# Attention with decay and a gated feed-forward layer: GpSimd's products kept away from VectorE's scaling, and ScalarE's casts spread out

## The chip, the cores and the metric

The kernel runs on one core of a Trainium2 chip. The metric is the device time of one execution in microseconds (us), as the median over runs. The engines are called as in the profile: PE is TensorE's matmul (PEld its weight load), DVE is VectorE, ACT is ScalarE, POOL is GpSimd, SP is SyncE.

## The reference

There are 8 batches of 8 heads with 576 positions of 64 numbers, so 4608 tokens of 512 numbers. A causal attention with a decay from running sums of `s` is followed by a normalization and a gated feed-forward layer:

```python
scores = scale * q @ k.T                              # per batch and head, scale = 1/8
cum    = cumsum(maximum(s, 0))
scores = where(causal, -1e9, scores + minimum(-(cum[i] - cum[j]), 0))
attn   = softmax(scores)
x      = (attn @ v) as rows of 512                    # 4608 x 512
xn     = x / sqrt(mean(x*x) + 1e-6) * rms_g
g      = xn @ w_gate                                  # 512 x 1536
out    = (g * sigmoid(g) * (xn @ w_val)) @ w_out      # 1536 x 512
```

## The kernel before

The feed-forward layer works in 9 chunks of 512 tokens, numbered 0 to 8. `ffn` emits a chunk. For each of 12 blocks of 128 columns it issues four matmuls for G (line 910), a tanh T on ACT (line 913), four matmuls for V (line 919), and on DVE first U from T and G (line 922), then Ht from U and V (line 915). After that come four output tiles of 12 matmuls each (line 932), taken out by ACT (line 937). G, V, the output tiles and part of the scores take turns in four PSUM buffers with the name `psF`, in the order in which they are asked for. A new G or V can therefore start only when the reader of the buffer's last use is done: for G's buffer that is U, for V's it is Ht.

The attention of the later batches is fitted in between by a planner that runs when the program is written. After every four matmuls of `ffn` it calls `step`, and each call is a slot, 36 of them in a chunk. In a slot the planner issues what is due by counts of slots alone. Nothing in it reacts to times on the chip. Each engine then works through its own instructions in the order in which they were issued, and waits at semaphores where data is not there.

For batches 4 to 7, a pair (b, c) is batch b and its block c of 128 positions. These are the steps that matter here:

- ScalarE casts Q to bf16 in five pieces (`cast_x`, lines 161 and 150). They stand in the queue `act_cast`. When all are done, SP's queue transposes K and Q piece by piece (`kq_dma`, line 189).
- A score run (`s_run`, matmuls of line 366) uses a `psF` buffer, a `psT` and a `psS`. In the next four slots ACT takes exponentials (line 379), and POOL sets the masked half to zero (line 383; for batches up to 3 it is line 318).
- POOL multiplies a block of V by the decay (`fold_b`, lines 402 and 405). I call this a fold. All tensors of it lie in SBUF.
- PE multiplies probabilities and V (`av_step`, lines 430 and 436), and DVE divides by the sums (lines 444 and 446), which gives a block of x.
- ACT squares the block and sums the squares (line 453). POOL makes the factor `al_all` out of the sum (`alpha`, lines 466 and 469). DVE scales the block by that factor and by `rms_g` (`x_scale`, line 476, inputs and output in SBUF). SP's queue transposes it into the feed-forward layer's input (line 487).

In `step` the parts come in this order: delayed work, one exponential, the scaling, casts on ACT, transposes, loads of V, then POOL's own queue or a fold, and last PE's work of the attention (`place`). The lines that decide on casts and folds are:

```python
        if not busy and not run_side(act_side) and last["run"] > 0:
            run_side(act_cast)
        ...
            if not run_side(pool_side) and phase() < 25 and not moved and fold_seq and ready(9, "V", *fold_seq[0]) and not (
                    scaled[0] < len(x_list) and ready(XLAG - 2, "AV", *x_list[scaled[0]], 1)):
                fold_b(*fold_seq.pop(0))
```

`ready(n, "AV", b, qb, 1)` is true from n slots after the second half of that block's product with V. `XLAG` is 6, `SQLAG` is 2, `MB` is 4. For batches up to 3 the factor is issued in the slot of the product; for later ones it comes three slots after it. `x_list[scaled[0]]` is the next block that DVE will scale.

Of the kernel before, what the change touches and what calls it, by code (L numbers as in the profile page):

```python
# [9 lines left out]
BF16 = mybir.dt.bfloat16  # L10
# [16 lines left out]
def kernel(  # L27
# [12 lines left out]
    nc = tc.nc  # L40
    B, H, S, D = q.shape
    DM = H * D
# [4 lines left out]
    NSC = 5  # L47
# [6 lines left out]
    def rows(c):  # L54
        return 128 if c < 4 else 64
# [14 lines left out]
    mp = fast.enter_context(tc.tile_pool(name="mp", bufs=1))  # L70
# [14 lines left out]
    MB = 4  # L85
    PERIOD, PACE, MLAG, XLAG, SQLAG = 9, 2, 1, 6, 2
# [4 lines left out]
    NX = 4  # L91
    x_sb = mp.tile([128, NX, DM], BF16, name="x_sb")
    xs_sb = mp.tile([128, NX, DM], BF16, name="xs_sb")
# [5 lines left out]
    g_col = mp.tile([128, CC], FP32, name="g_col")  # L99
    ss_all = mp.tile([128, B * NSC], FP32, name="ss_all")  # L100
    al_all = mp.tile([128, B * NSC], FP32, name="al_all")
    acc = mp.tile([128, 2560], BF16, name="acc")
    mag = mp.tile([128, H * 320], BF16, name="mag")
    s_sb = mp.tile([BH, S], FP32, name="s_sb")
# [12 lines left out]
    def psAV():  # L117
        return pp.tile([128, 512], FP32, name="psAV", tag="AV", bufs=1)
# [7 lines left out]
    def psT32():  # L126
        return pp.tile([128, 512], FP32, name="psT32", tag="T", bufs=1)
# [210 lines left out]
    def s_run(b, kb):  # L338
# [49 lines left out]
        def part(g, par):  # L388
            exps(g, par)
            if g:  # L390
                last[("RA", "RT")[par]] = slot[0]
            if par:
                after(MLAG, lambda: mask(g, kb, 0, 128))
                if join:
                    after(MLAG, lambda: mask(g, 4, 192, 64))

        last["RA"] = last["RT"] = 10 ** 6
        exp_q.extend((join, lambda a=(g, par): part(*a)) for g in (1, 0) for par in (0, 1))

    def fold_b(b, c):  # L400
        i = (b - MB) * H
        nc.gpsimd.tensor_tensor(
            out=v_sb[:, b % 2, c, :, 0:64], in0=v_sb[:, b % 2, c, :, 0:64],
            in1=vwx[:, c, i:i + H].unsqueeze(2).to_broadcast([128, H, 64]), op=ALU.mult)
        nc.gpsimd.tensor_copy(out=v_sb[:, b % 2, c, :, 64], in_=vwx[:, c, i:i + H])
        done["W", b, c] = slot[0]
# [6 lines left out]
    def part_of(b, qb):  # L413

        return slice(64, 128) if b >= MB and qb == 4 else slice(0, rows(qb))

    def av_step(b, qb, g, ps=None, act=False):
        p = b % 2
        if ps is None:
            ps = psT32() if 0 < b < MB and g == 1 else psAV()  # L420
        for j in range(4):
            h = 4 * g + j
            o = ps[:, j * NV:(j + 1) * NV]
            e, back, own = j, 128, 0
            if b >= MB:
                e = 2 * (j % 2) + j // 2
                if qb == 4:
                    back, own = 64, 128
            if qb > 0:
                nc.tensor.matmul(o, lhsT=E[:, eslot[b, qb - 1, g], e, back:back + 128],  # L430
                                 rhs=v_sb[:, p, qb - 1, h, :], start=(j == 0), stop=False)
            if qb < 4 or b >= MB:
                d = E[:, eslot[b, qb, g], e, own:own + 128]
            else:
                d = E[:, eslot[b, 4, 0]].rearrange("p h (a n) -> p (h a) n", n=128)[:, h, :]
            nc.tensor.matmul(o, lhsT=d, rhs=v_sb[:, p, qb, h, :],  # L436
                             start=(j == 0 and qb == 0), stop=(j == 3))
        if qb > 0:
            eread[eslot[b, qb - 1, g]] -= 1
        eread[eslot[b, qb, g if qb < 4 or b >= MB else 0]] -= 1  # L440
        R = part_of(b, qb)
        pv = ps[:, 0:4 * NV].rearrange("p (h e) -> p h e", e=NV)
        rZ = mp.tile([128, 4], FP32, name="rZ", tag="rZ", bufs=3)
        nc.vector.reciprocal(out=rZ[R], in_=pv[R, :, 64])  # L444
        xo = x_sb[R, (b * NSC + qb) % NX, :]
        nc.vector.tensor_tensor(  # L446
            out=xo[:, g * 256:(g + 1) * 256].rearrange("p (h d) -> p h d", h=4),
            in0=pv[R, :, 0:64], in1=rZ[R].unsqueeze(2).to_broadcast([R.stop - R.start, 4, 64]), op=ALU.mult)

        def norm(whole=True):  # L450
            col = b * NSC + qb
            if act:
                nc.scalar.activation(  # L453
                    out=xs_sb[R, (b * NSC + qb) % NX, :], in_=xo, func=AF.Square,
                    accum_out=ss_all[R, col:col + 1])
            else:
                nc.vector.scalar_tensor_tensor(
                    out=xs_sb[R, (b * NSC + qb) % NX, :], in0=xo, scalar=1.0, in1=xo,
                    op0=ALU.mult, op1=ALU.mult, accum_out=ss_all[R, col:col + 1])
            if whole:  # L460
                alpha(col, col + 1, R)
        return norm
# [58 lines left out]
    slot = [0]  # L521
    first, chunk = [0], [0]
    done = {}
    exp_q = []
    last = {"XS": -9, "P": -9, "RA": -9, "RT": -9, "run": -9, "S": -9, "AV": -9, "T": -9, "X": -9, "AVT": -9, "L": -9, "TT": -9, "TA": -9, "AVA": -9}
    s_seq = [(b, kb, g) for b in range(B) for kb in range(NSC) for g in (0, 1) if kb < 4 or g == 0]
    s_seq.sort(key=lambda x: (1, 0, x[2], x[1]) if x[0] == 1 and x[1] < 2 else (x[0], x[1], x[2], 0))
    s_seq = [x for x in s_seq if x[0] < MB or x[1] < 4 and x[2] == 0]
# [11 lines left out]
    pool_side, dve_side, v_side, act_side, act_cast = [], [], [], [], []  # L540
    x_seq = []
    fold_seq = [(b, c) for b in range(MB, B) for c in range(NSC)]

    def at(*key):
        return done.get(key, 10 ** 6)

    def ready(lag, *key):
        return at(*key) + lag <= slot[0]

    def run_side(queue):  # L550
        if queue and queue[0][0]():
            queue.pop(0)[1]()
            return True
        return False
# [22 lines left out]
    def phase():  # L577

        return slot[0] - first[0]
# [219 lines left out]
    def by_pe(b, qb):  # L799

        return b == 0 or (b, qb) in ((1, 2), (1, 3))
# [9 lines left out]
    scaled = [0]  # L811
    x_list = [(b, qb) for b in range(B) for qb in range(NSC)]
# [7 lines left out]
    def step(bare=False, tanh=False):  # L820

        slot[0] += 1
        while pending:
            pending.pop(0)()
        for x in [x for x in delayed if x[0] <= slot[0]]:
            delayed.remove(x)
            x[1]()
        busy = bool(exp_q) and phase() <= 24
        for _ in range(1):
            if exp_q:  # L830
                exp_q.pop(0)[1]()
        moved = False
        if scaled[0] < len(x_list):
            b, qb = x_list[scaled[0]]
            if ready(5 if (b, qb) == (1, 1) else XLAG if b >= MB else 3, "AV", b, qb, 1):
                x_scale(b, qb)
                last["XS"] = slot[0]
                scaled[0] += 1
                if not by_pe(b, qb):
                    assert xt_seq[0] == (b, qb)  # L840
                    xt_dma(*xt_seq.pop(0))
                    done["XT", b, qb] = slot[0] + 4
                    moved = True
        if not busy and not run_side(act_side) and last["run"] > 0:
            run_side(act_cast)

        if not moved and x_seq and slot[0] - last["X"] >= 2 and not (
                scaled[0] < len(x_list) and x_list[scaled[0]] != (1, 4) and ready(1 if x_list[scaled[0]][0] < MB else XLAG - 2, "AV", *x_list[scaled[0]], 1)):
            b, w, c = x_seq[0]
            old = ("R", b - 2, c) if b - 2 >= (XB if w else KB) else ("S", b - 2, 4, 0)  # L850
            if (ready(1 if b == 2 else 2, "cast", b, 1) and ready(1, *old)
                    and (w == 1 or ready(7, "K", b, c))):
                x_seq.pop(0)
                kq_dma(b, w, c)
                done["X", b, w, c] = last["X"] = slot[0]
                if b >= KB and (w, c) == (0, NSC - 1) and b + 2 < B:
                    casts(b + 2)
        bare = bare or chunk[0] == 0 and 30 <= phase() <= 33
        if slot[0] % 2 and not bare and not (chunk[0] == 0 and phase() >= 24):
            run_side(v_side)  # L860
        if not bare:
            if not run_side(pool_side) and phase() < 25 and not moved and fold_seq and ready(9, "V", *fold_seq[0]) and not (
                    scaled[0] < len(x_list) and ready(XLAG - 2, "AV", *x_list[scaled[0]], 1)):
                fold_b(*fold_seq.pop(0))
        place()
        if chunk[0] < 3 or last["AV"] < slot[0] and not moved:
            run_side(dve_side)
# [157 lines left out]
    with tc.manual_schedule():  # L1025
# [7 lines left out]
        for w in (0, 1):  # L1033
# [8 lines left out]
            out=mneg.rearrange("p (j n) -> p j n", j=2), in_=mneg.rearrange("p (j n) -> p j n", j=2),  # L1042
# [353 lines left out]
```

## Time and profile before

| | us |
|---|---|
| median of 3 runs | 364.1 |
| the runs | 364.74, 362.69, 364.10 |
| the profiled execution | 363.98 |
| its span, first to last instruction | 362.3 |
| PE busy in the span | 346.8 (96%) |
| DVE busy | 278.7 (77%) |
| ACT busy | 223.9 (62%) |
| POOL busy | 193.7 (53%) |

The span is what the profile's views divide up. In a row of the timeline the first number is the start in us from the span's beginning, the second the length, then engine, line, operation, and output<-input; an idle time before it and who ended it may stand in brackets. In a row of busy time by stretch come the stretch, its length, and the busy time of PE, PEld, DVE, ACT and POOL with the number of instructions, then the clock that PE was granted (1.00 is full speed), and the share and rate of the DMA.

### The profile page before, as it was taken

The page shows a single profiled execution, that of the slowest core. Times are in us where ns is not written, and L with a number is a line of the kernel's source. Part 1 is how long each engine was busy: PE and PEld are TensorE (multiplying, and loading weights), DVE is VectorE, ACT ScalarE, POOL GpSimd, SP SyncE. Part 2 cuts the span into 40 slices and gives each one's busy share as a digit, 9 for nine tenths or more (in the row PEclk, how much of TensorE's full clock was granted, in tenths as well). Part 3 has the DMA queues.
Part 4 walks back from the last instruction along what each step waited for, and adds up shares of the span by engine and source line. Part 5 has one row for each costly group of instructions (what it writes and reads, how often), then busy time and mean ns, then how long its engine had stood idle before and what let it go on. Part 6 is the DMA issues. An engine that isn't in the chain of part 4 may idle for free. (4 is left out here: it accounts for less than half of the span.)

```text
span 362.3 us, 6904 instructions
## 1 busy us (share of the span) xinstructions
PE 346.8 (96%) x2419; PEld 165.1 (46%) x2419; DVE 278.7 (77%) x524; ACT 223.9 (62%) x507; POOL 193.7 (53%) x310
## 2 busy tenths in 40 slices
PE   5989999999999999979999999999999999999993
PEld 2445444543444444434544444445444454444441
DVE  6797988698999888788769976997799359827820
ACT  3988885778787876845757845664666455223311
POOL 6959663738863878947583778565652210000000
PEclk9999999999999999989999999999999999999998
DMA  7999999999999599959996999299501221020011
GB/s 227 138 234 253 175 174 253 181 206 193 175 161 208 55 104 127 181 59 180 218 211 68 82 144 197 37 97 137 119 16 24 72 74 23 2 87 29 1 60 63
DMA packets 124800, 45.68 MB, mean 126 GB/s; under 512 B 103924, under 2 KB 119800, under 8 KB 124760
## 3 DMA queue, kind: packets, MB, share of 16 engines
q0 software_dynamic: 62368, 13.11, 45.2%
q1 hardware_dynamic: 51328, 23.67, 32.3%
q10 hardware_dynamic: 11064, 8.41, 9.9%
q8 instruction: 20, 0.33, 0.4%
q14 instruction: 20, 0.16, 0.2%
HBM read 37.90 MB, written 9.44 MB: 131 GB/s over the span
## 5 line engine op out<-in xcount | busy, mean ns | idle before, releaser
L919 PE MATMUL psF<-xnT,wv_sb 128*128 128x512 bf16 x432 | 111.9, 382 | 2.4 <-DVE U L922 2.4
L910 PE MATMUL psF<-xnT,wg_sb 128*128 128x512 bf16 x432 | 111.7, 381 | 0.3 <-ACT xnT L503 0.3
L913 ACT ACTIVATE T<-psF 128x512 f32<-128x512 f32 x108 | 64.4, 597 | 63.2 <-PE psF L910 60.7
L932 PE MATMUL psF<-wout_sb,Ht 128*128 128x512 bf16 x432 | 100.4, 379 | 0.0
L922 DVE SCALAR_TENSOR_TENSOR U<-T,psF 128x512 bf16<-128x512 f32 x108 | 73.8, 683 | 24.8 <-ACT T L913 22.7
L915 DVE TENSOR_TENSOR Ht<-U,psF 128x512 bf16<-128x512 bf16 x99 | 67.7, 684 | 6.1 <-PE psF L919 0.5
L919 PEld LDWEIGHTS <-wv_sb 128*128 128x128 bf16 x432 | 39.7, 98 | 47.4 <-issue 6.3
L932 PEld LDWEIGHTS <-Ht 128*128 128x128 bf16 x432 | 39.7, 98 | 44.4 <-issue 1.0
L910 PEld LDWEIGHTS <-wg_sb 128*128 128x128 bf16 x432 | 38.7, 98 | 41.4 <-issue 4.3
L937 ACT ACTIVATE osb<-psF 128x512 f32<-128x512 f32 x36 | 21.6, 600 | 48.3 <-PE psF L932 40.4
L309 ACT ACTIVATE E<-psS,biasK 128x256 bf16<-128x256 f32 (+3 forms) x136 | 44.7, 421 | 4.2 <-PE psS L285 4.0
L383 POOL TENSOR_SCALAR_AFFINE_SELECT E<-E 128x512 bf16<-128x512 bf16 (+1 forms) x40 | 24.9, 631 | 38.4 <-ACT E L379 35.7
L476 DVE SCALAR_TENSOR_TENSOR xs_sb<-x_sb,al_all,g_row 128x512 bf16<-128x512 bf16 (+1 forms) x36 | 31.4, 873 | 7.1 <-POOL al_all L469 6.8
L193 POOL DMA_DIRECT2D v_sb<-in_v_dram x40 | 35.2, 882 | 0.0
L318 POOL TENSOR_SCALAR_AFFINE_SELECT E<-E 128x512 bf16<-128x512 bf16 x28 | 19.3, 690 | 24.0 <-ACT E L309 23.3
L466 POOL TENSOR_SCALAR al_all<-ss_all 128x1 f32<-128x1 f32 (+2 forms) x39 | 10.7, 273 | 38.7 <-ACT xs_sb L453 31.0
L514 DVE TENSOR_TENSOR acc<-acc,mag 128x1280 bf16<-128x1280 bf16 x32 | 28.8, 923 | 0.3
L453 ACT ACTIVATE xs_sb<-x_sb 128x512 bf16<-128x512 bf16 (+1 forms) x37 | 23.2, 627 | 7.8 <-DVE x_sb L446 6.9
L446 DVE TENSOR_TENSOR x_sb<-psAV,rZ 128x256 bf16<-128x256 f32 (+1 forms) x61 | 25.9, 424 | 2.1
L436 PEld LDWEIGHTS <-E 128*128 128x128 bf16 x320 | 21.9, 98 | 10.4 <-issue 0.8
L469 POOL TENSOR_TENSOR al_all<-al_all,mhalf 128x1 f32<-128x1 f32 (+2 forms) x39 | 24.7, 633 | 3.2
L444 DVE RECIPROCAL rZ<-psAV 128x4 f32<-128x4 f32 (+1 forms) x61 | 10.9, 179 | 18.8 <-PE psAV L436 18.4
(135 smaller groups left out, 392.8 us busy)
## 6 DMA issues: line engine op xcount, KB each, us to landing
out_dram<-osb SPq DMA_DIRECT2D x36, 256.0 KB, 2.3
kq<-in_q_dram ACTq DMA_DIRECT2D x5, 1024.0 KB, 7.8
v_sb<-in_v_dram POOLq DMA_DIRECT2D x32, 128.0 KB, 4.8
kq<-in_k_dram SPq DMA_DIRECT2D x4, 512.0 KB, 5.8
kq<-in_q_dram SPq DMA_DIRECT2D x4, 512.0 KB, 7.6
kq<-in_k_dram ACTq DMA_DIRECT2D x2, 1024.0 KB, 9.3
kqn<-in_k_dram POOLq DMA_DIRECT2D x16, 128.0 KB, 4.9
wout_sb<-in_moe_w_out_dram POOLq DMA_DIRECT2D x2, 768.0 KB, 10.5
```

The source lines that it names most:

```text
L193: nc.gpsimd.dma_start(out=v_sb[0:n, b % 2, c, :, 0:64], in_=v[b, :, c * 128:c * 128 + n, :].rearrange("h p d -> p h d"))
L309: nc.scalar.activation(out=eo, in_=ei, func=AF.Exp, scale=0.125, bias=biasK[:, kb, bh:bh + 1])
L383: nc.gpsimd.affine_select(out=Ev, in_=Ev, pattern=[[0, 4], [1, nq]], compare_op=ALU.is_ge, fill=0.0, base=0, channel_multiplier=-1)
L446: nc.vector.tensor_tensor(out=xo[:, g * 256:(g + 1) * 256].rearrange("p (h d) -> p h d", h=4), in0=pv[R, :, 0:64], in1=rZ[R].unsqueeze(2). ...
L476: nc.vector.scalar_tensor_tensor(out=xs_sb[R, (b * NSC + qb) % NX, :], in0=x_sb[R, (b * NSC + qb) % NX, :], scalar=al_all[R, col:col + 1], ...
L514: nc.vector.tensor_tensor(out=acc[:, sl], in0=acc[:, sl], in1=mag[:, sl], op=ALU.max)
L910: nc.tensor.matmul(Gp, lhsT=wg_sb[:, cc, fs], rhs=xnT[:, cc, x0:x0 + DM], start=(cc == 0), stop=(cc == CC - 1))
L913: nc.scalar.activation(out=T, in_=Gp, func=AF.Tanh, scale=0.5)
L915: nc.vector.tensor_tensor(out=Ht[:, fb - 1, :], in0=pend[0], in1=pend[1], op=ALU.mult)
L919: nc.tensor.matmul(Vp, lhsT=wv_sb[:, cc, fs], rhs=xnT[:, cc, x0:x0 + DM], start=(cc == 0), stop=(cc == CC - 1))
L922: nc.vector.scalar_tensor_tensor(out=U, in0=T, scalar=1.0, in1=Gp, op0=ALU.add, op1=ALU.mult)
L932: nc.tensor.matmul(Op, lhsT=Ht[:, fb, tb * 128:(tb + 1) * 128], rhs=wout_sb[:, fb, :], start=(fb == 0), stop=(fb == FB - 1))
```

## The change

Three things change in `step`.

- A fold is no longer issued between a block's factor and its scaling. For a block of batches up to 3, folds are held back from the slot after its product with V; for later ones from two slots after it (it was four slots after, for all).
- A fold that is issued less than four slots after a scaling has a small copy ahead of it on POOL. The copy reads one element of the scaled row, so POOL waits there until DVE has done that scaling. 19 of the 20 folds have one.
- ScalarE's casts of Q are issued in every second slot at most, and not in the slot of a square sum or the one after. Before, they could go in each slot.

```diff
+    probe = mp.tile([128, 1], BF16, name="probe")
...
+    def behind_scale():
+        b, qb = x_list[scaled[0] - 1]
+        r0 = part_of(b, qb).start
+        nc.gpsimd.tensor_copy(out=probe[r0:r0 + 1], in_=xs_sb[r0:r0 + 1, (b * NSC + qb) % NX, DM - 1:DM])
...
             if act:
+                last["SQ"] = slot[0]
                 nc.scalar.activation(
...
-        if not busy and not run_side(act_side) and last["run"] > 0:
-            run_side(act_cast)
+        if not busy and not run_side(act_side) and last["run"] > 0 and slot[0] - last["C"] > 1 and slot[0] - last["SQ"] > 1:
+            if run_side(act_cast):
+                last["C"] = slot[0]
...
-            if not run_side(pool_side) and phase() < 25 and not moved and fold_seq and ready(9, "V", *fold_seq[0]) and not (
-                    scaled[0] < len(x_list) and ready(XLAG - 2, "AV", *x_list[scaled[0]], 1)):
+            if not run_side(pool_side) and phase() < 25 and not moved and fold_seq and ready(
+                    9, "V", *fold_seq[0]) and not (scaled[0] < len(x_list) and ready(
+                        0 if x_list[scaled[0]][0] < MB else SQLAG, "AV", *x_list[scaled[0]], 1)):
+                if slot[0] - last["XS"] < 4:
+                    behind_scale()
                 fold_b(*fold_seq.pop(0))
```

Since all later decisions of the planner follow from earlier ones, the order of the attention's instructions differs from the first fold of batch 4 on (chunk 3) to the end of chunk 7. The instructions are the same, apart from the 19 copies.

More of the change, by code (lines that the diff above doesn't have):

```diff
@@ L524 @@
     exp_q = []
-    last = {"XS": -9, "P": -9, "RA": -9, "RT": -9, "run": -9, "S": -9, "AV": -9, "T": -9, "X": -9, "AVT": -9, "L": -9, "TT": -9, "TA": -9, "AVA": -9}
+    last = {"C": -9, "SQ": -9, "XS": -9, "P": -9, "RA": -9, "RT": -9, "run": -9, "S": -9, "AV": -9, "T": -9, "X": -9, "AVT": -9, "L": -9, "TT": -9, "TA": -9, "AVA": -9}
     s_seq = [(b, kb, g) for b in range(B) for kb in range(NSC) for g in (0, 1) if kb < 4 or g == 0]
```

## The prediction

> **What bounds the kernel now.** I read the page's first two parts, then the busy time chunk by chunk, then the chain of waits, then the timeline around the one wait of TensorE that matters.
>
> ```profile
> span 362.3 us, 6904 instructions
> PE 346.8 (96%) x2419; PEld 165.1 (46%) x2419; DVE 278.7 (77%) x524; ACT 223.9 (62%) x507; POOL 193.7 (53%) x310
> PEclk9999999999999999989999999999999999999998
> ```
> TensorE (PE) is the bound: 96% busy, and the granted clock dips in one slice in the middle. The change adds and removes no matmul, so it can win only where PE idles or is slowed. The chunks say where (PE busy is the first figure after the length):
>
> ```profile
> 145.10:184.90 39.80, 37.38 (x251) 17.68 (x250) 31.56 (x51) 25.21 (x53) 28.16 (x45) 0.96 1.24 168
> 184.90:221.00 36.10, 36.09 (x266) 17.56 (x264) 29.70 (x55) 23.40 (x48) 25.36 (x39) 1.00 1.14 122
> 221.00:257.20 36.20, 36.20 (x267) 17.60 (x266) 29.95 (x55) 20.86 (x43) 23.31 (x39) 1.00 0.98 111
> ...
> PE psF L919 <- DVE U L922: 2.4, 1, 2.4
> ```
> The chunks from 184.9 on have PE filled. The chunk from 145.1, the first that the edits reach, has 2.42 us of idle PE and a mean clock of 0.96. The last line, from the chain of waits, is that idle time: one wait, by the V matmuls of line 919 for the U of line 922 on VectorE (DVE). The timeline there, engine by engine:
>
> ```profile
> 150.74 1.03 PE L910 MATMUL psF<-xnT,wg_sb 128*128 128x512 bf16 x4
> 152.47 1.03 PE L910 MATMUL psF<-xnT,wg_sb 128*128 128x512 bf16 x4
> 153.43 0.28 PE L366 MATMUL psF<-kqT 64*128 64x256 bf16 x1
> ...
> 153.66 0.38 PE L366 MATMUL psS<-kqT 64*128 64x256 bf16 x4
> 156.46 1.02 PE L919 MATMUL psF<-xnT,wv_sb 128*128 128x512 bf16 x4 [2.42 <-DVE U L922]
> ...
> 152.03 0.69 DVE L915 TENSOR_TENSOR Ht<-U,psF 128x512 bf16<-128x512 bf16 x1
> 152.63 3.18 DVE L476 SCALAR_TENSOR_TENSOR xs_sb<-x_sb,al_all,g_row 64x512 bf16<-64x512 bf16 x1
> 155.74 0.67 DVE L922 SCALAR_TENSOR_TENSOR U<-T,psF 128x512 bf16<-128x512 f32 x1
> ...
> 151.40 0.21 POOL L405 CAST v_sb<-vwx 128x8 bf16<-128x8 f32 x1
> 151.70 0.18 POOL L466 TENSOR_SCALAR al_all<-ss_all 64x1 f32<-64x1 f32 x1
> 151.97 0.56 POOL L469 TENSOR_TENSOR al_all<-al_all,mhalf 64x1 f32<-64x1 f32 x1
> 152.50 0.62 POOL L383 TENSOR_SCALAR_AFFINE_SELECT E<-E 128x512 bf16<-128x512 bf16 x1
> 153.10 1.03 POOL L402 TENSOR_TENSOR v_sb<-v_sb,vwx 128x512 bf16<-128x512 bf16 x1
> 154.09 0.21 POOL L405 CAST v_sb<-vwx 128x8 bf16<-128x8 f32 x1
> 154.24 1.03 POOL L402 TENSOR_TENSOR v_sb<-v_sb,vwx 128x512 bf16<-128x512 bf16 x1
> 155.22 0.67 POOL L405 CAST v_sb<-vwx 128x8 bf16<-128x8 f32 x1
> ```
> PE stood from 153.66 + 0.38 = 154.04 to 156.46. U was behind the scaling of line 476, x(3,4), which took 3.18 us. All that time GpSimd (POOL) ran back to back: a mask, then two products of V and decay ("folds", lines 402 and 405). Is it POOL that stretches the scaling?
>
> ```profile
> L476 DVE SCALAR_TENSOR_TENSOR xs_sb<-x_sb,al_all,g_row x36: 737/748/3179, 41.9 to 305.0; 128x512 bf16<-128x512 bf16 x28, 64x512 bf16<-64x512 bf16 x8
> L476 DVE SCALAR_TENSOR_TENSOR xs_sb<-x_sb,al_all,g_row 64x512 bf16<-64x512 bf16 x8 | 8.5, 1065 | 0.1
> 59.85 1.04 DVE L476 SCALAR_TENSOR_TENSOR xs_sb<-x_sb,al_all,g_row 128x512 bf16<-128x512 bf16 x1
> 59.71 0.64 POOL L318 TENSOR_SCALAR_AFFINE_SELECT E<-E 128x512 bf16<-128x512 bf16 x1
> 256.27 1.52 DVE L476 SCALAR_TENSOR_TENSOR xs_sb<-x_sb,al_all,g_row 128x512 bf16<-128x512 bf16 x1 [1.09 <-POOL al_all L469]
> 256.21 1.04 POOL L402 TENSOR_TENSOR v_sb<-v_sb,vwx 128x512 bf16<-128x512 bf16 x1
> ```
> The median is 748 ns. Long ones began just after a POOL instruction, and end a fixed time after it: 60.89 against 60.35, 257.79 against 257.25, and 155.81 against the second fold's 155.27: 0.54 us each. So a scaling that finds POOL at work waits, and under a back-to-back POOL stream waits again and again. The 64-row form is not slow by itself: (8.5 − 3.18) / 7 = 0.76 us.
>
> The Trainium skill, page "SBUF — State Buffer", section "Who interferes with whom", says that VectorE with two SBUF inputs and GpSimd's reads exclude each other for a whole instruction, and that whoever issues first has the port. The waiting agrees (3.18 us). The order doesn't: by that rule the scaling, there since 152.63, follows the mask at 153.12 and the folds cost it nothing; here two folds went ahead of it.
>
> Next, the clock. The last row is another place, with PE's busy time alone:
>
> ```profile
> 154.40:157.80 3.40, 1.34 (x7) 0.62 (x7) 3.30 (x4) 0.84 (x2) 2.39 (x3) 0.99 0.14 24
> 157.80:161.20 3.40, 3.40 (x13) 1.37 (x12) 2.33 (x5) 1.57 (x3) 1.21 (x2) 0.50 0.83 77
> 86.70:90.10 3.40, 2.75 (x18) 1.00 2.60 125
> ```
> Straight after the stretch with 1.34 us of busy PE, the clock is 0.50 for 3.4 us: half of that, 1.7 us, is lost. A stretch with 2.75 us busy was at 1.00 and no drop followed. So the one stall costs 2.42 + 1.7 = 4.1 us, the most that there is to win.
>
> **The change part by part.** Made against the profiled execution, 363.98 us (span 362.3, and 1.7 around it). The three runs are 364.74, 362.69 and 364.10, median 364.1; their spread of 2.05 is about one half-clock stretch, so I guess that some runs miss it.
>
> *Folds kept out and tied.* In the changed order of instructions folds (4,3) and (4,4) move from chunk 3's slots 5 and 10 to slots 8 and 10, behind the scaling of x(3,4) in slot 7. Each of 19 folds gets a one-element copy ahead of it; that copy reads the scaled row, so POOL waits for the scaling. Folds (4,0) to (4,2) stay ahead of the factor, now with three copies. A copy's price isn't in the trace; the nearest rows:
>
> ```profile
> L405 POOL CAST v_sb<-vwx x20: 207/219/695, 148.5 to 264.3; 128x8 bf16<-128x8 f32 x20
> 0.43 0.10 POOL L1380 MEMSET const-float32-0.0<- 128x1 f32 x1 [0.43 <-issue]
> L922 DVE SCALAR_TENSOR_TENSOR U<-T,psF x108: 667/686/690, 28.2 to 345.7; 128x512 bf16<-128x512 f32 x108
> ```
> 0.10 to 0.30 us (a cast plus a wait); I take 0.2, near the cast. None can be below nothing, being added work in order. The copies' own waits are over here: x(3,3) was scaled slots before.
>
> Step by step: the factor ended at 151.97 + 0.56 = 152.53, straight behind fold (4,2); three copies make that 153.13. The mask is next on POOL and again comes just ahead (152.50 was 0.03 before 152.53): 153.10 to 153.72. The scaling waits for it and ends 0.54 later, 154.26. Behind the mask POOL now waits, so nothing starves the scaling. U starts 0.07 before that (155.74 against 155.81), 154.19, takes 0.67, ends 154.86; V follows 0.05 later, as 156.46 followed 156.41: 154.91. The stall shrinks from 2.42 to 0.87: **1.55 us won**. With copies at 0.10 or 0.30, V is at 154.61 or 155.21: 1.25 to 1.85. Should the scaling beat the mask, it lasts 0.75 from about 153.2, V is at 154.6: inside that.
>
> *The half clock.* With 0.87 us idle, a 3.4 us stretch keeps about 2.5 us busy: near 2.75 (no drop), far from 1.34 (drop). I count it gone: **1.7 us won**.
>
> *Casts of Q in every second slot.* These rows are ScalarE's (ACT):
>
> ```profile
> 151.11 1.14 ACT L161 ACTIVATE kqn<-kq 128x512 bf16<-128x512 f32 x2
> 152.15 0.58 ACT L913 ACTIVATE T<-psF 128x512 f32<-128x512 f32 x1
> 153.67 0.58 ACT L913 ACTIVATE T<-psF 128x512 f32<-128x512 f32 x1
> ```
> Its input was done at 150.74 + 1.03 = 151.77, but T ran at 152.15 behind two casts; with one it can run some 0.3 earlier. That wins nothing here: U waits for the scaling. The end at the gain side is 0.3 if the scaling weren't there; at the loss side, the casts finish later. Batch 5's end in slot 26 instead of 9, its first transposes on SP's queue go out in slot 30 instead of 20, and each score run from (5,0) on stands three slots later (from chunk 3's slot 36 to chunk 4's slot 3). Two slots take 152.47 − 150.74 = 1.73 us, so that is 2.6 us later. Every planned transpose still goes out five slots or more before its run, that is 4.3 us. The last scaling, x(7,4), goes from slot 12 of chunk 7 to slot 16; chunk 8 begins after slot 36. I cost it at nothing; the cover is PE's own queue of feed-forward matmuls. If it is gone, a run waits for its transposes.
>
> Sum: 363.98 − 1.55 − 1.7 = 360.73, so **360.7 us**.
>
> **The rivals.**
>
> *The half clock stays, 362.4 us.* Only the 1.55 goes. For it: 0.87 us of idle time lies between a stretch that drew a drop and one that drew none, and where a stretch begins is open. Against: 2.75 us busy drew no drop. The Trainium skill, "TensorE: Matmul & The Clock Gate", section "What's actually happening", has a free-running window of about 3.4 us, with the clock halved after an idle window; the length agrees (3.4 us at 0.50), but a window with 1.34 us busy wasn't idle. Taken strictly, the stall didn't cause the drop and it would stay.
>
> *Nothing stretches less, 364.0 us.* If the scaling's wait is not the folds' but the mask's and DVE's own, U is late as before. Against: the 0.54 behind the last fold.
>
> *POOL becomes late, 368.9 us.* In chunks 5 and 6 the scaling is in slot 3, and three to four tied folds, two masks and the next factor queue behind it, up to the scaling in slot 12. In chunk 6: the scaling ends 3 × 0.865 + 0.75 = 3.3 us in; folds go at 154.24 − 153.10 = 1.14 each, three of the four with a copy, 5.2 in all; masks 2 × 0.62; factor 152.53 − 151.70 = 0.83: 10.6 us. Slot 12 is at 12 × 0.865 = 10.4 plus 0.6 for a run (here 153.43 to 154.04), 11.0. That is 0.4 us of room, and the U behind it has about a slot, 0.9, before its buffer is wanted. From about 1.3 us of further lateness on, PE would stand; at a stall with its half clock, 4.1 us, in both chunks: 363.98 − 3.25 + 8.2 = 368.9.
>
> *All of it goes, 359.9 us.* Copies near free and no mask in the way: 363.98 − 4.1.
>
> **How the numbers follow.** Forecast 0.60, half clock stays 0.12, all goes 0.12, nothing changes 0.07, POOL late 0.09. 0.5% is 1.8 us, about what a measurement can tell. Faster: forecast and all gone, 0.72. Within: half clock stays and nothing changes, 0.19. Slower: 0.09. The range takes in the first three: 359.6 (all gone, with some spread of the runs) to 362.8 (half clock, with the dearer copies).
>
> **What would show it.** Right: the scaling of x(3,4) at about 1.1 us with one mask ahead; PE's wait for U at 0.6 to 1.2 us; no slice at half clock; POOL standing behind copies. Wrong: a scaling over 1.5 us, a clock of 0.50 after a shorter stall, or a new wait of PE for U or for a transpose past 185 us.

## The result, and the profile after

| | us |
|---|---|
| changed kernel, median of 7 runs | 361.49 (361.09 to 362.57) |
| kernel before, median of 7 runs, the three known ones among them | 363.55 (362.34 to 364.74) |
| ratio | 0.9951, 95% interval 0.9928 to 0.9974 |
| profiled execution of the changed kernel | 362.57, span 360.9 |

The forecast was 360.7 with 359.6 to 362.8. Measured again on two chips of the experiments (e6 and e10), the change came out at 0.9986 (0.9964 to 1.0008) and 0.9956 (0.9935 to 0.9976). So it is a gain of half a percent at most, in one of three measurements none that can be told from nothing, and about half or less of the 4.1 us that there were to win. The profiled execution was the longest of the seven. In the page of the changed kernel (line numbers are shifted: x's scaling is L484, U is L934, V is L931, a run's matmuls L367, a transpose of K and Q L190; the small copy is L405, a fold L409, the factor L477, the mask L384):

```profile
span 360.9 us, 6884 instructions
PE 342.5 (95%) x2374; PEld 164.8 (46%) x2419; DVE 275.2 (76%) x524; ACT 223.6 (62%) x507; POOL 196.3 (54%) x329
PEclk9999999999999999999999999999999999999999
```
No slice shows a lower clock any more. (Here 45 matmul records are missing, so PE's busy time can't be set against the one before; the engine has the same 2419 weight loads.) PE's waits from 145 us on, by the chain of waits of that stretch:

```profile
PEld L367 <- DMA kqT<-kqn: 1.7, 2, 1.3
PE psF L367 <- DMA kqT<-kqn: 1.0, 1, 1.0
PE psF L367 <- ACT T L925: 0.7, 1, 0.7
PE psF L931 <- DVE U L934: 0.7, 1, 0.7
```
The wait for U is down from 2.4 to 0.7. The other three lines are all at the runs of line 367; before, the only line of that kind from 145 us on was 0.4 us of PEld, in which PE itself did not stand. The timeline shows the first place engine by engine, and then the two new ones:

```profile
153.87 0.38 PE L367 MATMUL psS<-kqT 64*128 64x256 bf16 x4
154.91 1.02 PE L931 MATMUL psF<-xnT,wv_sb 128*128 128x512 bf16 x3 [0.66 <-DVE U L934]
...
153.16 1.11 DVE L484 SCALAR_TENSOR_TENSOR xs_sb<-x_sb,al_all,g_row 64x512 bf16<-64x512 bf16 x1 [0.23 <-POOL al_all L477]
154.19 0.67 DVE L934 SCALAR_TENSOR_TENSOR U<-T,psF 128x512 bf16<-128x512 f32 x1
...
150.87 0.18 POOL L405 COPY probe<-xs_sb 1x1 bf16<-1x1 bf16 x1
151.01 1.03 POOL L409 TENSOR_TENSOR v_sb<-v_sb,vwx 128x512 bf16<-128x512 bf16 x1
152.56 0.56 POOL L477 TENSOR_TENSOR al_all<-al_all,mhalf 64x1 f32<-64x1 f32 x1
153.09 0.63 POOL L384 TENSOR_SCALAR_AFFINE_SELECT E<-E 128x512 bf16<-128x512 bf16 x1
154.33 0.18 POOL L405 COPY probe<-xs_sb 1x1 bf16<-1x1 bf16 x1 [0.61 <-DVE xs_sb L484]
154.47 1.03 POOL L409 TENSOR_TENSOR v_sb<-v_sb,vwx 128x512 bf16<-128x512 bf16 x1
...
180.06 1.22 SPq L190 DMA_TRANSPOSE kqT<-kqn  x1
184.09 3.78 SPq L190 DMA_TRANSPOSE kqT<-kqn  x2
182.31 0.37 ACTq L137 DMA_DIRECT2D kq<-in_q_dram  x1
184.93 0.27 PE L367 MATMUL psF<-kqT 64*128 64x256 bf16 x1 [0.70 <-ACT T L925]
194.74 0.27 PE L367 MATMUL psF<-kqT 64*128 64x256 bf16 x1 [1.05 <-DMA kqT<-kqn]
```
Between the factor and the scaling there is now only the mask. The scaling lasts 1.11 us instead of 3.18, POOL stands at the copy for 0.61 us, and V begins at 154.91.

The new waits are the score runs (5,0) and (5,1) at the head of chunk 4. Their last transposes were issued at 180.06 and from 184.09 on; by the trace they landed 4.7 and 9.8 us after issue, at 184.8 and 193.9 at the earliest. The runs began at 184.93 and 194.74. So the line that names T is best read as the same wait for a transpose: in the profile of e10 below, T had ended 0.2 us before that run began, and there the wait is put down to the transpose. (Of the four matmuls ahead of the second gap one has no record, so about 0.2 us of the 1.05 is work.) The load of batch 7's Q, 1 MB, was issued at 182.31 in their midst.

In the plan of slots the reason is plain. Before, each run stood 10 or more slots behind its last transpose, (5,0) and (5,1) 12 and 14. In the changed kernel these two have 5 and 8, and the others of batch 5 have 8: the casts of Q end later, so the transposes go out later.

### The profile page after: what moved, and what is told of

Same layout as the page of the kernel before. It is cut to its first block, busy times and chain, and to the rows that moved or that the text cites. A ratio compares the mean times of both kernels' runs of the same rounds, so it can differ in the third digit from the quotient of the medians.

```text
span 360.9 us, 6884 instructions
## 1 busy us (share of the span) xinstructions
PE 342.5 (95%) x2374; PEld 164.8 (46%) x2419; DVE 275.2 (76%) x524; ACT 223.6 (62%) x507; POOL 196.3 (54%) x329
## 5 line engine op out<-in xcount | busy, mean ns | idle before, releaser
L931 PE MATMUL psF<-xnT,wv_sb 128*128 128x512 bf16 x422 | 110.0, 379 | 1.1 <-DVE U L934 0.7
L922 PE MATMUL psF<-xnT,wg_sb 128*128 128x512 bf16 x416 | 109.4, 379 | 1.0 <-ACT xnT L511 0.3
L944 PE MATMUL psF<-wout_sb,Ht 128*128 128x512 bf16 x416 | 98.2, 379 | 0.8
L934 DVE SCALAR_TENSOR_TENSOR U<-T,psF 128x512 bf16<-128x512 f32 x108 | 73.6, 682 | 30.3 <-ACT T L925 29.6
L931 PEld LDWEIGHTS <-wv_sb 128*128 128x128 bf16 x432 | 39.4, 98 | 45.5 <-issue 4.6
L384 POOL TENSOR_SCALAR_AFFINE_SELECT E<-E 128x512 bf16<-128x512 bf16 (+1 forms) x40 | 25.5, 647 | 32.3 <-ACT E L380 29.3
L484 DVE SCALAR_TENSOR_TENSOR xs_sb<-x_sb,al_all,g_row 128x512 bf16<-128x512 bf16 (+1 forms) x36 | 28.6, 795 | 5.7 <-POOL al_all L477 5.4
L522 DVE TENSOR_TENSOR acc<-acc,mag 128x1280 bf16<-128x1280 bf16 x32 | 27.9, 890 | 0.3
L477 POOL TENSOR_TENSOR al_all<-al_all,mhalf 128x1 f32<-128x1 f32 (+2 forms) x39 | 25.8, 662 | 3.2
L443 PEld LDWEIGHTS <-E 128*128 128x128 bf16 x320 | 21.8, 98 | 10.1 <-issue 0.2
L437 PEld LDWEIGHTS <-E 128*128 128x128 bf16 x256 | 20.1, 98 | 7.7 <-DVE x_sb L453 0.6
```

Source lines behind the costliest of these rows:

```text
L477: nc.gpsimd.tensor_tensor(out=al_all[R, c0:c1], in0=al_all[R, c0:c1], in1=mhalf[R, 0:c1 - c0], op=ALU.pow)
L484: nc.vector.scalar_tensor_tensor(out=xs_sb[R, (b * NSC + qb) % NX, :], in0=x_sb[R, (b * NSC + qb) % NX, :], scalar=al_all[R, col:col + 1], ...
L522: nc.vector.tensor_tensor(out=acc[:, sl], in0=acc[:, sl], in1=mag[:, sl], op=ALU.max)
L922: nc.tensor.matmul(Gp, lhsT=wg_sb[:, cc, fs], rhs=xnT[:, cc, x0:x0 + DM], start=(cc == 0), stop=(cc == CC - 1))
L931: nc.tensor.matmul(Vp, lhsT=wv_sb[:, cc, fs], rhs=xnT[:, cc, x0:x0 + DM], start=(cc == 0), stop=(cc == CC - 1))
L934: nc.vector.scalar_tensor_tensor(out=U, in0=T, scalar=1.0, in1=Gp, op0=ALU.add, op1=ALU.mult)
```

## The experiments

My theory after the result (A): the folds' part wins what was forecast, and the casts' part gives some 2 us back. Rival (B): the casts are neutral, and the new waits belong to that one execution. All ratios below are to the kernel before, run on the same chip. They are taken over all runs of both kernels, and can differ by some 0.2% from the quotient of the medians.

**Folds alone, casts alone, and folds without their tie** (one chip).

```diff
 e1: the change, but
-        if not busy and not run_side(act_side) and last["run"] > 0 and slot[0] - last["C"] > 1 and slot[0] - last["SQ"] > 1:
-            if run_side(act_cast):
-                last["C"] = slot[0]
+        if not busy and not run_side(act_side) and last["run"] > 0:
+            run_side(act_cast)
 e2: the kernel before, with that edit the other way round
 e3: e1, but
-                if slot[0] - last["XS"] < 4:
-                    behind_scale()
```

> The changed kernel with the casts of Q put back to every slot; folds held out and tied as changed. Theory A (the cast part gives back some 2 us, because the score runs of batch 5 now reach their transposes): the runs stand where they stood before, 12 or more slots behind their last transpose, so PE waits for no transpose and the time is 359.0 to 360.0 us. Rival B (the casts are neutral, and the two waits for transposes in the changed kernel's profile belong to that one execution, the slowest of seven): 361.2 to 361.8 us, as the changed kernel. Both: the scaling of x(3,4) at 1.1 us.

> The kernel before with nothing but the casts of Q in every second slot. A: the scaling of x(3,4) still lasts about 3.2 us and the runs of batch 5 wait for transposes as well, so 1.5 to 2.5 us above the kernel before, about 365.5 us. B: as the kernel before, 363.6 us.

> As the folds-only kernel, but without the copies that tie a fold behind the scaling; folds (4,3) and (4,4) are still issued after it, in slots 8 and 10. If POOL's stream is what keeps the scaling waiting, the mask and then these two folds follow the factor at once: the scaling of x(3,4) lasts 3 us or more again, PE waits 2 us or more, about 363.5 us. Rival (the later slots do it, the copies are idle weight): scaling 1.1 us, and the time of the folds-only kernel or 0.2 us less.

Folds alone: 361.19 us, ratio 0.9934 (0.9912 to 0.9955). By the time alone that is rival B (361.2 to 361.8), and 1.2 us above what A had said. The profile is as A had it: no run waits for a transpose, and from 145 us on PE has this one wait for another engine:

```profile
PE psF L930 <- DVE U L933: 0.7, 1, 0.7
```
Which of the two holds is decided further down, where both kernels run on one chip (e6 and e8).

Casts alone: 364.02 us, 1.002 (0.9989 to 1.0051). The runs' waits are there, and so is the old stall (U is L924 here):

```profile
PE psF L921 <- DVE U L924: 2.4, 1, 2.4
PEld L366 <- DMA kqT<-kqn: 1.7, 2, 1.3
PE psF L366 <- DMA kqT<-kqn: 1.6, 2, 1.0
```
By the time alone it is not set apart from the kernel before; by the waits it is A, at less than A's price.

Without the tie: 363.06 us, 1.000 (0.9975 to 1.0025). The later slots alone won nothing:

```profile
PE psF L928 <- DVE U L931: 2.4, 1, 2.4
...
152.82 3.17 DVE L484 SCALAR_TENSOR_TENSOR xs_sb<-x_sb,al_all,g_row 64x512 bf16<-64x512 bf16 x1
...
152.15 0.56 POOL L477 TENSOR_TENSOR al_all<-al_all,mhalf 64x1 f32<-64x1 f32 x1
152.68 0.62 POOL L384 TENSOR_SCALAR_AFFINE_SELECT E<-E 128x512 bf16<-128x512 bf16 x1
153.29 1.03 POOL L409 TENSOR_TENSOR v_sb<-v_sb,vwx 128x512 bf16<-128x512 bf16 x1
154.27 0.21 POOL L412 CAST v_sb<-vwx 128x8 bf16<-128x8 f32 x1
154.42 1.03 POOL L409 TENSOR_TENSOR v_sb<-v_sb,vwx 128x512 bf16<-128x512 bf16 x1
```
The two folds are issued one and three slots behind the scaling, but nothing on POOL's own queue makes them wait for it. They follow the mask at once, and the scaling waits for all of them, as before. This kernel and the folds alone differ by the copies and by nothing else, so the stall's cause is shown: POOL's stream. The two scalings, 3.17 and 1.11 us, differ by 2.06.

The twelve runs of e3 also show the clock. Six lie between 362.06 and 362.73, five between 364.16 and 365.00, one at 363.39; the means of the two groups, 362.47 and 364.46, are 2.0 apart. Those of e1 lie from 360.49 to 361.87 without a gap. In the profiles, busy time by stretch (PE first, the clock is the number after POOL's), e3:

```profile
154.10:157.50 3.40, 0.93 (x7) 0.48 (x5) 3.30 (x4) 1.33 (x3) 2.87 (x5) 1.00 0.26 51
157.60:161.00 3.40, 3.40 (x13) 1.28 (x12) 2.27 (x5) 1.57 (x3) 0.45 (x1) 0.50 0.85 79
```
and e2, the same stall of 2.4 us:

```profile
154.90:158.30 3.40, 1.39 (x6) 0.68 (x7) 3.19 (x5) 0.12 (x1) 2.29 (x3) 1.00 0.14 23
158.30:161.70 3.40, 3.40 (x25) 1.68 (x23) 3.23 (x8) 2.64 (x5) 1.48 (x2) 1.00 0.81 76
```
In e3 the half clock follows, in e2 it doesn't. So the stall brings the half clock in some executions only, about half of them by the groups of e3.

**The load among the transposes** (same chip).

```diff
-                    loads(b + 2, 1, early, 28 if b == KB else 4)
+                    loads(b + 2, 1, early, 28 if b == KB else 22)
```

> The changed kernel with the load of batch 7's Q (1 MB) moved from slot 1 to slot 14 of chunk 4, so that it is no longer issued among batch 5's transposes. If it is that load that makes them land late (up to 9.8 us after issue), PE's waits in the runs (5,0) and (5,1), together 1.9 us in the profile, go: 359.4 to 360.2 us. If the room of 5 and 8 slots is too short by itself: 361.2 to 361.8 us, with the waits still there.

362.94 us, 0.9978 (0.9954 to 1.0002). Neither: the waits for transposes are 2.2 (PE) and 2.0 us (PEld) in this profile, and the time is above both ranges.

```profile
PE psF L367 <- DMA kqT<-kqn: 2.2, 2, 1.4
PEld L367 <- DMA kqT<-kqn: 2.0, 2, 1.6
```
PE stands at the run (5,0) for 0.8 us, and not at (5,1), but 1.4 us at (5,3), from 212.2 us on. The load went out at 199.81 here. The first transpose for (5,1), issued at 184.55, landed after 5.0 us; beside the load it was 9.8. Those issued at 205.5 and 206.8, behind the load's new place, took 7.5 and 8.1 us; in the profiles of the change (result, e6 and e10) a transpose issued there landed after 3.5 to 3.9. So the load does delay transposes, and moving it moved the wait. The last transpose for (5,0) landed 4.9 us after issue with that load some 20 us away, so with its five slots (4.3 us) that run is late without the load.

**The factor first, and the change against folds alone on one chip.** The wait of 0.7 us that is left starts with POOL: fold (4,2) ran from 151.01 ahead of the factor.

```diff
 e5: e1, and
-                        0 if x_list[scaled[0]][0] < MB else SQLAG, "AV", *x_list[scaled[0]], 1)):
+                        0 if x_list[scaled[0]][0] < MB else SQLAG, "AV", *x_list[scaled[0]], 1)) and not (
+                            av_seq and av_seq[0] == (MB - 1, 4, 1) and can_av()):
 e6: the changed kernel
 e7: the changed kernel, with ready(10, "X", ...) for ready(5, "X", ...) in run_ready
 e8: e1 again
```

> The folds-only kernel, with fold (4,2) held back from chunk 3's slot 4 as well, so that POOL makes the factor of x(3,4) without it in front; the fold goes to slot 8 behind the scaling. In the folds-only profile PE still stands 0.66 us for the U behind that scaling. If the factor's lateness is what is left: the scaling ends about 1.2 us earlier, PE's wait is under 0.1 us, and the time is 0.5 to 0.7 us under the folds-only kernel of the same chip, about 360.5 us. Rival (fold (4,2) pushes folds (4,3) and (4,4) and what follows on POOL, or U waits for T at that point): PE's wait stays at 0.4 us or more, or a new one comes, and the time is that of the folds-only kernel.

> The changed kernel once more, on the same chip as the folds-only kernel. Theory A: PE waits for transposes in the runs of batch 5 in this profile too, 1 us or more together, and the time is 0.8 to 2 us above the folds-only kernel. Rival (those waits were one execution's): no such wait, and the two within 0.3 us.

> The changed kernel with score runs held until 10 slots after their last transpose (it was 5): the run (5,0) goes to slot 8 of chunk 4, the next ones follow. If the late casts cost only by the runs' waits for transposes: no such wait in the profile, and the time of the folds-only kernel within 0.4 us. Rival (late casts cost in other ways, or the later runs crowd products and scalings): 0.8 us or more above it.

> The folds-only kernel once more, as the measure for the three others on this chip: 360.8 to 361.5 us, PE's one wait for U near 0.7 us.

| kernel | median us | ratio, 95% interval |
|---|---|---|
| e5, factor first | 360.42 | 0.9917 (0.9887 to 0.9947) |
| e6, the change | 362.34 | 0.9986 (0.9964 to 1.0008) |
| e7, ten slots of room | 362.77 | 0.9999 (0.9971 to 1.0026) |
| e8, folds alone | 361.09 | 0.9940 (0.9913 to 0.9967) |

Spacing the casts costs 362.34 − 361.09 = 1.25 us here, inside A's expectation. In e6's profile only the run (5,0) held PE up, for 0.7 us (the first line again names T):

```profile
PE psF L367 <- ACT T L925: 0.7, 1, 0.7
PE psF L931 <- DVE U L934: 0.7, 1, 0.7
PEld L367 <- DMA kqT<-kqn: 0.4, 1, 0.4
```
That execution took 361.52, under the median, so the wait seems to change from one execution to the next; that the runs' waits are the whole 1.25 us isn't shown. e7 doesn't decide: its runs wait for no transposes, but being later they made the planner put in 9 more matmuls, to keep PE at work while it waits for x at the end of chunk 4 (9 × 0.216 = 1.9 us). e5 is 0.67 under e8, as much as e8's wait for U, and in its profile no such wait is left.

**Less room than that, and the best version again** (a third chip).

```diff
 e9: the changed kernel, with ready(7, "X", ...) for ready(5, "X", ...) in run_ready
 e10: the changed kernel
 e11: e5 again
```

> The changed kernel with score runs held until 7 slots after their last transpose (it was 5; 10 made the planner add 9 warm-up matmuls, 7 adds none). The run (5,0) goes to slot 5 of chunk 4, the rest of batch 5 stands 10 or more slots behind its transposes. If the late casts cost by the runs' waits alone: no wait for a transpose over 0.3 us in the profile, and 0.7 to 1.9 us under the changed kernel of the same chip. Rival (they cost otherwise): the time of the changed kernel within 0.4 us.

> The changed kernel as the measure on this chip: 361.4 to 362.4 us, with a wait of a run for transposes in the profile.

> The kernel with casts in every slot, folds tied, and fold (4,2) behind the scaling, once more: no wait of PE over 0.1 us between 145 us and the end, 360.2 to 360.7 us, 1 to 2 us under the changed kernel of the same chip.

The change: 361.74 us, 0.9956 (0.9935 to 0.9976). Two slots more: 361.24, 0.9964 (0.9935 to 0.9993). Factor first: 359.87, 0.9918 (0.9891 to 0.9944). In e10 the run (5,0) stood again:

```profile
PE psF L367 <- DMA kqT<-kqn: 0.9, 1, 0.9
PE psF L931 <- DVE U L934: 0.7, 1, 0.7
```
In e9 that wait is gone, but (5,1) waits 0.5 us. That is neither of the two forecasts: the median is 0.5 lower than e10's, the ratio is not, and that more room alone buys the casts' cost back isn't shown. In e11 PE has no gap:

```profile
145.00:181.00 36.00, 36.00 (x253) 17.23 (x250) 28.75 (x51) 25.50 (x53) 28.32 (x52) 1.00 1.38 168
181.00:217.00 36.00, 36.00 (x265) 17.57 (x264) 29.70 (x55) 23.30 (x47) 23.73 (x41) 1.00 1.23 141
217.00:253.00 36.00, 36.00 (x266) 17.52 (x264) 29.75 (x55) 20.63 (x43) 21.71 (x40) 1.00 1.04 112
...
152.67 0.74 DVE L484 SCALAR_TENSOR_TENSOR xs_sb<-x_sb,al_all,g_row 64x512 bf16<-64x512 bf16 x1
151.12 0.56 POOL L477 TENSOR_TENSOR al_all<-al_all,mhalf 64x1 f32<-64x1 f32 x1
151.65 0.62 POOL L384 TENSOR_SCALAR_AFFINE_SELECT E<-E 128x512 bf16<-128x512 bf16 x1
```
The factor ends at 151.68, 1.2 us earlier than in e10 (152.88); the mask is over before DVE comes to the scaling, and that takes 0.74 us. The two profiles differ by 1.6 us from chunk 3's first matmul to the last matmul (208.6 against 207.0), and e10's two waits above make 1.6. At 359.87 e11 lies 0.3 under its forecast. This version, casts as before and the factor ahead of fold (4,2), beats both kernels: 0.8% under the kernel before on two chips, 1.9 us under the change.

## Why the prediction was right, and where not

It was right in the direction and the range, with 361.49 in 359.6 to 362.8 and 0.8 above the forecast. Two of its terms were off, both toward too much gain: the half clock, and the casts. The forecast gain was 363.98 − 360.73 = 3.25 us; the medians give 363.55 − 361.49 = 2.06. The time came nearer than the gain because the forecast started from an execution 0.4 over the median of before, and that is luck. With the terms as measured below (1.76 for the stall, 0.7 for the half clock, less 1.25 for the casts) the gain would be 1.2 us; the three measurements of the change lie around that: 2.06 here, 0.4 and 1.3 by the medians on the two chips of e6 and e10.

*The scaling's stall: right to the step.* Forecast were a factor pushed back by three copies, a mask ahead of the scaling, 0.54 us from the mask's end to the scaling's, and V at 154.91. It was 154.91. That is partly luck: the chunk began 0.2 later (G at 152.69, not 152.47), and a copy takes 0.14 to 0.15 from its start to the fold's instead of 0.2. The mask ended at 153.72 and the scaling at 154.27, 0.55 later. PE's wait is 0.66, forecast 0.87. e3 shows that the copies make the difference, e11 that the mask and fold (4,2) are the rest.

The rule of the Trainium skill, page "SBUF — State Buffer", section "Who interferes with whom", that whoever issues first gets the port, again didn't give the order: in e3 the scaling was there from 152.82, and folds that began at 153.29 and 154.42 both went ahead of it.

*The half clock: counted in full, but it comes in less than half of the executions.* The step that failed is "I count it gone: 1.7 us won", set against one execution that had it and read as a step of the median. It was gone, but the times of before hold only part of it. Every run was recorded with its mean granted clock, and a half clock of 3.4 us takes about 0.005 off it (1.7 of 362). Of the 87 runs of the kernel before on the three chips of the experiments, 37 show 0.994 or less, all of them at 363.61 us or more; of the other 50, 48 took 363.57 us or less. With that share the term is some 0.7 instead of 1.7. None of the changed kernel's 31 runs shows so low a clock. The guess that some runs miss it was in the text and didn't go into the sum.

The Trainium skill, page "TensorE: Matmul & The Clock Gate", section "What's actually happening", says that the window runs free. The profiles agree. In before the drop begins at 157.77 us and the clock falls once more at the kernel's end, at 359.15; in e3 it is 157.56 and 358.95. In both profiles 201.4 us lie between, 59 times 3.41, so the drops stand on a grid. In e2 the end's fall is at 359.71, and 60 such steps earlier is 154.9, where the stretch shown for it begins. The stall of 2.4 us began at 154.45 there, 0.5 us ahead of that stretch, and drew no half clock; in e3 it lay wholly in one stretch and drew one (in before 0.3 us of it lay ahead, and it drew one too). That the window has to be idle is not borne out: the clock dropped after 1.34 us of busy PE. The rival, that the half clock stays, was wrong: none of the profiles with the wait at 0.7 us or less has one.

*The casts: costed at nothing, measured at 1.25 us on one chip.* The failed step is "Every planned transpose still goes out five slots or more before its run, that is 4.3 us", taken as cover. Transposes landed 4.7 and 9.8 us after issue. The row to look at was the time to landing in the profile of before, and not the planner's distance alone:

```profile
L189 SPq DMA_TRANSPOSE kqT<-kqn x50: 1182/1231/2054, 68.4 to 260.4; - x50
...
DMA to landing us min/median/max: 2.3/4.3/8.5
```
So the cover of 4.3 us was no more than the median of that row (the three numbers are the least, the median and the most). The text named the wait that comes if the cover goes, and among its signs of being wrong a wait of PE for a transpose past 185 us, which came; but no rival was made of it. That POOL becomes late, the rival that was made, didn't happen: from 203 us on each scaling lasted 0.74 to 0.77 us, and PE waited for none of them.

*The sum of the two profiled executions.* Spans: 362.3 − 1.76 (stall) − 1.7 (half clock) + 1.5 (the two runs' waits, 0.7 and some 0.8) is 360.3; measured 360.9. Of the 0.6 that is left, 0.2 was there ahead of the first changed instruction: the scaling of x(3,3) began at 146.38 instead of 146.17. The other 0.4 is open.

## What to carry to other kernels

An instruction that is issued later isn't one that runs later: on another engine's queue only a wait keeps it there, and a one-element copy is such a wait for about 0.15 us. A distance counted in slots covers a transfer only as far as its slowest landing, and when producers are moved, the distance of each consumer should be counted again. What one profiled execution shows of a clock drop goes into a forecast of the median with the share of executions that have it.

## What was not expected of the hardware

- The waiting scaling got in neither between the mask and a fold nor between a fold's two instructions, but behind the second fold, where POOL's cast then took 0.67 us instead of 0.21. Three runs show it at the same place (3.18, 3.17 and 3.17 us). Why there is open.
- Where the clock tips is narrow by these rows: 1.34 us of busy PE in 3.4 drew the half clock, 1.39 did not; PE's busy time is modelled, so the two numbers only say that they lie close.
- A transpose issued 1.8 us behind a 1 MB load from another queue landed 9.8 us later, and 5.0 us later with that load moved away (e4); the median over the kernel's 50 is 3.7.
